# Attention and a dense mixture of experts on one core: on-chip transposes in place of a trip through memory, casting loads from GpSimd, and more of the first expert beside the attention

## The chip, the core and the metric

The kernel runs on one core of a Trainium2 chip. TensorE (PE) does matrix products and transposes and writes PSUM only; PEld is its weight load. VectorE (DVE) and ScalarE (ACT) read PSUM and write SBUF; GpSimd (POOL) works on SBUF. DMA transfers are issued from the queues of SyncE (SP), ACT or POOL and run on 16 DMA engines. The metric is the device time of one execution, in microseconds; lower is better.

## The reference

Four batches of eight heads, 768 positions, 64 numbers a head. Each position attends to a band of 31 neighbours and to 24 block summaries (the maximum of each block of 32 keys, the mean of its values, with a weight of 32). The result, 3072 rows of 512, goes through eight experts, every one on every row, weighted by a matrix P that eight rounds of row and column scaling (Sinkhorn) make from the gate's logits.

```python
mask_l = np.abs(pos[:, None] - pos[None, :]) < window          # window 16
scores_s = scale * np.einsum('bhsd,bhnd->bhsn', q, k_sum) + np.log(block)
...
x = np.ascontiguousarray(attn_out.transpose(0, 2, 1, 3)).reshape(B * S, H * D)
logits = x @ w_gate
P = np.exp(logits)
for _ in range(8):
    P /= P.sum(1, keepdims=True) + 1e-09
    P /= P.sum(0, keepdims=True) + 1e-09
    P *= N / E
for e in range(E):
    out += P[:, e:e + 1] * (np.maximum(x @ w1[e], 0.0) @ w2[e])
```

## The kernel before

**Attention** runs over 16 pairs of heads (`NPAIR`), four pairs to a batch, 128 positions to a tile, six tiles (`G`) to a head. `load_pair` issues six loads of 192 KB in fp32 from SP's queue, two pairs ahead: q, k and v of two heads, 768 rows of 256 bytes each. `cast_qk` and `cast_v` turn them into bf16 on DVE. `transpose_pair` makes 12 transposes on PE; DVE and ACT copy the results out of PSUM, and DVE takes the blockwise maximum of the keys (`ksumT`, L242). `head_scores` makes the band's scores (`sg`, L255, 158 columns a tile) and the summaries' (`ss`, L266); ACT takes exponentials (L260, L271). `head_mask` cuts the band out on POOL (L278). `head_vsum` (L288) sums the values by block. `head_av` (L310), for the pair before, makes 22 small products a head; DVE divides (L313, L314) into `x_sb`.

**The way to the experts.** After four pairs `store_batch` writes the batch's 768 x 512 result to a buffer in device memory, `x_bridge`, and `xbar_batch` reads it back transposed by four DMA transposes into `xT` (L327). `logits_batch` makes the gate's logits.

**Experts.** One step is 512 rows of one expert, six steps (`NG`) an expert, 48 in all. `mm1` makes eight groups of four 512-column matmuls (`hps`, L129) from the pool `fpsum`, which has two buffers, and ACT (L135) and DVE (L138) take turns to apply the relu into `hT`; `mm2` makes four groups of eight (`yps`, L451) for the step before, and DVE adds each group, times P, to `out_acc` (L462). The first two `mm1` of expert 0 (`PREFILL`) are dealt out in small pieces (`mm1_drip`, L149) between the last nine pairs of heads. Weights come in fp32 over SP's queue into one staging buffer (`wst`, 2 MB) and are cast by ACT (L117) or DVE (L119). The Sinkhorn rounds are dealt out over expert 0's steps.

**What sets the order.** Each engine has one queue in order. The code is written pair by pair, and a scheduler in the framework then sets the order within each queue; semaphores between engines do the rest. A DMA's issue waits on its own queue until its buffer is free, and every eighth issue waits for the transfer eight before it.

Of the kernel before, what the change touches and what calls it, by code (L numbers as in the profile page):

```python
# [13 lines left out]
AX = mybir.AxisListType  # L14


@with_exitstack
def kernel(
# [20 lines left out]
    NG = N // 512  # L39
    SCALE = 1.0 / float(D) ** 0.5  # L40
    WIN = 192
    LIVE = 158
    EPL = 112
    EW = EPL + WIN + 80
    NPAIR = (B * H) // 2

    PREFILL = 2
# [3 lines left out]
    dram = ctx.enter_context(tc.tile_pool(name="dram", bufs=1, space=bass.MemoryType.DRAM))  # L51
    fpsum = ctx.enter_context(tc.tile_pool(name="fpsum", bufs=2, space=bass.MemoryType.PSUM))
# [3 lines left out]

    band = const.tile([128, WIN], BF16)
    nc.gpsimd.memset(band, 1.0)
    nc.gpsimd.affine_select(out=band, in_=band, compare_op=ALU.is_ge, fill=0.0,
                            base=-1, pattern=[[1, WIN]], channel_multiplier=-1)  # L60
    nc.gpsimd.affine_select(out=band, in_=band, compare_op=ALU.is_ge, fill=0.0,
                            base=31, pattern=[[-1, WIN]], channel_multiplier=1)

    MBW = 148
    m_big = const.tile([128, MBW], BF16)
    nc.gpsimd.memset(m_big, 1.0)
    nc.gpsimd.affine_select(out=m_big, in_=m_big, compare_op=ALU.is_ge, fill=0.0,
                            base=640, pattern=[[-32, MBW]], channel_multiplier=1)
    nc.gpsimd.affine_select(out=m_big, in_=m_big, compare_op=ALU.is_ge, fill=0.0,
                            base=-609, pattern=[[32, MBW]], channel_multiplier=-1)  # L70
# [17 lines left out]
    wst = [persist.tile([128, 4096], FP32, name=f"wst{i}") for i in range(1)]  # L88
    w1_a = persist.tile([128, KD * F], BF16)
    w2_a = persist.tile([128, KF * DM], BF16)  # L90
    hT_sb = [persist.tile([128, KF, 512], BF16, name=f"hT{i}") for i in range(2)]
    nc.gpsimd.memset(crec_sb, 0.0)

    x_dram = dram.tile([N, DM], BF16, name="x_bridge")

    nc.scalar.dma_start(out=wg_f32[:], in_=moe_w_gate.rearrange("(dk p) e -> p dk e", p=128))
    nc.gpsimd.tensor_copy(out=wg_bf[:], in_=wg_f32[:])

    def load_w1(e, st, part=None):
        src = moe_w1[e].rearrange("(dk p) f -> p dk f", p=128)  # L100
        if part is None:
            nc.sync.dma_start(out=wst[st][:], in_=src)
        else:
            nc.sync.dma_start(out=wst[st][:].rearrange("p (dk f) -> p dk f", dk=KD)[:, part, :],
                              in_=src[:, part, :])

    def load_w2(e, st, part=None):
        src = moe_w2[e].rearrange("(fk p) d -> p fk d", p=128)
        if part is None:
            nc.sync.dma_start(out=wst[st][:], in_=src)  # L110
        else:
            nc.sync.dma_start(out=wst[st][:].rearrange("p (fk d) -> p fk d", fk=KF)[:, 2 * part:2 * part + 2, :],
                              in_=src[:, 2 * part:2 * part + 2, :])

    def cast_w(st, dst, eng):
        if eng is nc.scalar:
            nc.scalar.copy(out=dst[:], in_=wst[st][:])  # L117
        else:
            eng.tensor_copy(out=dst[:], in_=wst[st][:])  # L119

    w1x = [w1_a, None]
    w2x = [w2_a, None]
    hfill = [None]

    def mm1(e, n, fpool, eng2):
        for f in range(KF):
            hp = fpool.tile([128, 512], FP32, tag="h", name="hps")
            for dk in range(KD):
# [348 lines left out]
    for si, (e, n) in enumerate(steps):  # L477
# [14 lines left out]
        if si > 0:  # L492
            mm2(*steps[si - 1])
# [38 lines left out]
```

The softmax here doesn't subtract the row's maximum and nothing guards it: scores larger than these inputs give would overflow.

## Time and profile before

| what | us |
|---|---|
| median of 4 runs | 846.74 (844.48 to 850.33) |
| the profiled execution, its own time | 845.81 |
| its span, first to last instruction | 844.1 |
| last pair's result in `x_sb`, chain | 173.5 |
| `mm1` and `mm2` of one full step, chain | 7.14 and 6.91 |

The profiled execution's time is 1.7 us over its span, and 0.1% under the median. The page cuts the span in 40 slices of 21.1 us: busy shares in tenths, the granted TensorE clock (9 and more is the 2.4 GHz level), and the DMA engines' share. The attention is the first eight or nine slices. The views "by form" group instructions of one line and shape; the chain of waits follows the end of the program back to what released it.

### The profile page before, as it was taken

The page shows a single profiled execution, that of the slowest core. Times are in us where ns is not written, and L with a number is a line of the kernel's source. Part 1 is how long each engine was busy: PE and PEld are TensorE (multiplying, and loading weights), DVE is VectorE, ACT ScalarE, POOL GpSimd, SP SyncE. Part 2 cuts the span into 40 slices and gives each one's busy share as a digit, 9 for nine tenths or more (in the row PEclk, how much of TensorE's full clock was granted, in tenths as well). Part 3 has the DMA queues.
Part 4 walks back from the last instruction along what each step waited for, and adds up shares of the span by engine and source line. Part 5 has one row for each costly group of instructions (what it writes and reads, how often), then busy time and mean ns, then how long its engine had stood idle before and what let it go on. Part 6 is the DMA issues. An engine that isn't in the chain of part 4 may idle for free.

```text
span 844.1 us, 11265 instructions
## 1 busy us (share of the span) xinstructions
PE 788.8 (93%) x4608; PEld 385.7 (46%) x4608; DVE 403.4 (48%) x623; ACT 221.0 (26%) x434; POOL 78.1 (9%) x85
## 2 busy tenths in 40 slices
PE   2876887689999999999999999999999999999998
PEld 1655565544444444444444444444444444444443
DVE  6763676457645445444454454444544544444443
ACT  2644455512131111311311113113111131111110
POOL 6543344400000000000000000000000000000000
PEclk9975698679999999999999999999999999999999
DMA  9979688562022002200220022002200200001122
GB/s 175 173 190 201 161 195 192 142 170 105 0 101 100 1 0 100 100 1 0 100 100 1 0 100 101 1 0 100 100 1 0 101 1 1 0 1 50 55 96 100
DMA packets 107876, 65.76 MB, mean 78 GB/s; under 512 B 89392, under 2 KB 92464, under 8 KB 107824
## 3 DMA queue, kind: packets, MB, share of 16 engines
q1 hardware_dynamic: 104944, 64.43, 27.5%
q10 hardware_dynamic: 2880, 0.61, 0.5%
q8 instruction: 36, 0.59, 0.3%
q14 instruction: 16, 0.13, 0.0%
HBM read 52.45 MB, written 9.44 MB: 73 GB/s over the span
## 4 chain that ended last, share of the span: by engine, by line
PE 85%; DVE 6%; ACT 3%; DMA 2%; issue 2%; SPq 1%; POOL 0%; ACTq 0%; DVEq 0%; POOLq 0%
PE hps L129 38%; PE yps L451 37%; PE av L310 3%; PE hps L149 2%; DMA vvf<-in_v_dram 2%; PE ss L266 1%; PE tk L237 1%; PE sg L255 1%; PE tq L235 1%; DVE kkb L227 1%; ACT kkT L239 1%; DVE ksumT L242 1%; PE vs L288 1%; DVE qqb L226 1%; ACT Esum L271 1%
## 5 line engine op out<-in xcount | busy, mean ns | idle before, releaser
L135 ACT ACTIVATE hT<-hps 128x512 bf16<-128x512 f32 x184 | 109.5, 597 | 496.4 <-PE hps L129 484.3
L451 PEld LDWEIGHTS <-hT 128*128 128x128 bf16 x1536 | 150.1, 98 | 181.0 <-issue 2.7
L138 DVE TENSOR_SCALAR hT<-hps 128x512 bf16<-128x512 f32 x184 | 127.2, 691 | 190.9 <-PE hps L129 190.9
L462 DVE SCALAR_TENSOR_TENSOR out_acc<-yps,P_sb,out_acc 128x512 f32<-128x512 f32 x168 | 125.9, 751 | 153.5 <-PE yps L451 153.5
L129 PE MATMUL hps<-xT,w_b 128*128 128x512 bf16 x768 | 175.9, 378 | 0.3 <-ACT hT L135 0.2
L451 PE MATMUL yps<-w_a,hT 128*128 128x512 bf16 x768 | 174.4, 382 | 0.9 <-DVE xsb L314 0.9
L451 PE MATMUL yps<-w_b,hT 128*128 128x512 bf16 x768 | 170.0, 379 | 0.0
L129 PE MATMUL hps<-xT,w_a 128*128 128x512 bf16 x704 | 163.2, 378 | 0.3 <-DVE hT L138 0.2
L129 PEld LDWEIGHTS <-w_b 128*128 128x128 bf16 x768 | 74.4, 97 | 97.5 <-issue 17.6
L129 PEld LDWEIGHTS <-w_a 128*128 128x128 bf16 x704 | 67.8, 97 | 88.5 <-issue 16.3
L278 POOL TENSOR_TENSOR Et<-Et,band 128x948 bf16<-128x948 bf16 x32 | 66.6, 2083 | 89.7 <-ACT Et L260 88.8
L310 PE MATMUL av<-vsum,Esum 128*128 128x65 bf16 x192 | 34.4, 219 | 10.8 <-DVE xsb L314 7.3
L310 PE MATMUL av<-vve,Et 128*128 128x65 bf16 x512 | 39.0, 220 | 1.0 <-POOL Et L278 1.0
L310 PEld LDWEIGHTS <-Et 128*128 128x128 bf16 x512 | 32.3, 115 | 8.5 <-issue 6.2
L260 ACT ACTIVATE Et<-sg 128x316 bf16<-128x316 f32 x96 | 34.9, 427 | 3.6 <-PE sg L255 3.0
L255 PE MATMUL sg<-qqT,kkT 64*128 64x158 bf16 x192 | 27.7, 292 | 5.2 <-ACT kkT L239 4.9
L266 PE MATMUL ss<-qqT,ksumT 64*128 64x384 bf16 x64 | 23.2, 421 | 6.4 <-DVE ksumT L242 2.9
L271 ACT ACTIVATE Esum<-ss 32x384 bf16<-32x384 f32 x64 | 27.2, 475 | 7.1 <-PE ss L266 7.1
L235 PE MATMUL tq<-ident,qqb 128*128 128x128 bf16 x96 | 11.6, 276 | 17.8 <-DVE qqb L226 17.8
L310 PEld LDWEIGHTS <-Esum 128*128 128x128 bf16 x192 | 21.8, 114 | 13.1 <-PE av L310 7.6
L313 DVE RECIPROCAL recip<-av 128x6 f32<-128x6 f32 x32 | 6.2, 194 | 39.7 <-PE av L310 39.5
L226 DVE CAST qqb<-qqst 128x768 bf16<-128x768 f32 x16 | 22.9, 1433 | 4.2 <-DMA qqst<-in_q_dram 4.2
(73 smaller groups left out, 324.2 us busy)
## 6 DMA issues: line engine op xcount, KB each, us to landing
wst<-in_moe_w_dram SPq DMA_DIRECT2D x14, 2048.0 KB, 8.2
qqst<-in_q_dram SPq DMA_DIRECT2D x32, 192.0 KB, 4.0
out_dram<-out_acc SPq DMA_DIRECT2D x24, 256.0 KB, 2.0
vvf<-in_v_dram SPq DMA_DIRECT2D x31, 192.0 KB, 4.3
kkst<-in_k_dram SPq DMA_DIRECT2D x30, 192.0 KB, 4.0
wst<-in_moe_w_dram SPq DMA_DIRECT2D x8, 512.0 KB, 4.9
x_bridge<-xsb SPq DMA_DIRECT2D x4, 768.0 KB, 5.3
kkst<-in_k_dram ACTq DMA_DIRECT2D x2, 192.0 KB, 5.4
```

The costliest lines, as they stand in the source:

```text
L129: nc.tensor.matmul(hp[:], lhsT=w1x[e % 2][:, dk * F + f * 128:dk * F + (f + 1) * 128], rhs=xT[:, dk, n * 512:(n + 1) * 512], start=(dk == ...
L135: nc.scalar.activation(out=hT_sb[n % 2][:, f, :], in_=hp[:], func=AF.Relu, bias=0.0, scale=1.0)
L138: eng2.tensor_scalar_max(out=hT_sb[n % 2][:, f, :], in0=hp[:], scalar1=0.0)
L226: nc.vector.tensor_copy(out=qq_bf[i % 2][:], in_=qq_st[i % NQKB][:])
L255: nc.tensor.matmul(sg[:, gg, 1:1 + LIVE], lhsT=ktile[p0:p0 + 64, g * 128:(g + 1) * 128], rhs=qtile[p0:p0 + 64, g * 128 + 1:g * 128 + 1 + L ...
L260: nc.scalar.activation(out=et[:, 2 * gp:2 * gp + 2, EPL + 1:EPL + 1 + LIVE], in_=sg[:, :, 1:1 + LIVE], func=AF.Exp, bias=0.0, scale=SCALE)
L266: nc.tensor.matmul(ss[:, :], lhsT=ksumT[i % NTRB][p0:p0 + 64, :], rhs=qtile[p0:p0 + 64, 16 + half * 384:16 + (half + 1) * 384], start=True ...
L271: nc.scalar.activation(out=esum[0:32, half * 384:(half + 1) * 384], in_=ss[0:32, :], func=AF.Exp, bias=0.0, scale=SCALE)
L278: nc.gpsimd.tensor_tensor(out=et[:, :, EPL + 1:EPL + 1 + LIVE], in0=et[:, :, EPL + 1:EPL + 1 + LIVE], in1=band[:, None, 1:1 + LIVE].to_bro ...
L310: nc.tensor.matmul(av[:, c, :], lhsT=lhsT, rhs=rhs, start=(mi == 0), stop=(mi == len(mms) - 1))
L451: nc.tensor.matmul(yp[:], lhsT=hT_sb[n % 2][:, f, t4 * 128:(t4 + 1) * 128], rhs=w2x[e % 2][:, f * DM:(f + 1) * DM], start=(f == 0), stop=( ...
L462: nc.vector.scalar_tensor_tensor(out=out_acc[:, t, :], in0=yp[:], scalar=psl, in1=out_acc[:, t, :], op0=ALU.mult, op1=ALU.add)
```

## The change

The way of one pair is rewritten, and three things move between engines.

- **Loads**: `load` and `load_w` issue from POOL's queue (`nc.gpsimd.dma_start`) with a bf16 destination, so that the transfer casts. The casts on DVE and ACT and the staging buffers go. Pairs still come two ahead, now with three buffers. Expert 0's weights are queued behind pair 3's loads (`gate`), expert 1's behind pair 6's.
- **The mask** goes from POOL to DVE, four instructions a pair (L230), three tiles each.
- **The bridge** through memory goes. `to_xT` transposes a pair's result on PE, six transposes, and ACT copies 128 x 768 into `xT`.
- **Scores**: the two heads of a pair take turns (partitions 0 to 63 and 64 to 127), and the four `ss` products write four strips of 32 partitions of one tile, so one exponential of 128 x 384 takes the place of four of 32 x 384. The block sums of v are made for both heads at once.
- **Fill**: once a batch's `xT` is there, expert 0's whole work on that batch (two halves of 384 rows: eight `hidden` groups and three `project` groups each) is dealt out six pieces a pair through the next four pairs. Three of four batches of expert 0 so lie beside the attention.
- **Experts**: `hidden` draws from `mps2`, four PSUM buffers, `project` from `mps`, three. The Sinkhorn steps lie between the pieces of expert 0's last batch and expert 1's first two steps.

Two places in the queues. The loads: before, on SP's queue, from the end of batch 2 on:

```order
L321 DMA x_bridge<-xsb_151 128x6x512
L211 DMA qqst_113<-in_q_dram 128x6x64
L214 DMA kkst_115<-in_k_dram 128x6x64
L327 DMA_TRANSPOSE xT<-x_bridge 128x768 x4
L211 DMA qqst_113<-in_q_dram 128x6x64
L214 DMA kkst_115<-in_k_dram 128x6x64
L218 DMA vvf_117<-in_v_dram 128x6x64 x2
L112 DMA wst_94<-in_moe_w_dram 128x2x512
```

Now, on POOL's queue, from pair 3's loads on (`w_305` and `w_306` are expert 0's weights, the two copies are the gate):

```order
L183 DMA kst<-in_k_dram 128x6x64 x2
L183 DMA qst<-in_q_dram 128x6x64 x2
L186 DMA vx_112<-in_v_dram 128x6x64 x2
L109 COPY w_305<-kst 1x1
L110 COPY w_306<-kst 1x1
L183 DMA kst<-in_k_dram 128x6x64
L111 DMA w_305<-in_moe_w_dram 128x4x1024
L112 DMA w_306<-in_moe_w_dram 128x8x512
L183 DMA kst<-in_k_dram 128x6x64
```

The loads of q, k and v and the weights have moved from SP's queue to POOL's; pair 4's stand behind 4 MB of weights, and the bridge is gone from between them. The second place is DVE in the middle of the attention, one pair. Before:

```order
L226 CAST qqb_118<-qqst_112 128x768
L227 CAST kkb_120<-kkst_114 128x768
L313 RECIPROCAL recip_147<-av 128x6
L238 COPY qqT_126<-tq 128x384
L314 TENSOR_TENSOR xsb_150<-av,recip_147 128x6x64
L158 TENSOR_SCALAR hT_97<-hps 128x256
L240 COPY qqT_126<-tq 128x384
L242 TENSOR_REDUCE ksumT_132<-kkT_129 128x24
L223 CAST vve_123<-vvf_116 128x780
```

Now (`E_108`, `E_109` are the two heads' exponentials, `h` and `out_acc` belong to the fill):

```order
L230 TENSOR_TENSOR E_108<-E_108,band 128x3x158
L230 TENSOR_TENSOR E_109<-E_109,band 128x3x158
L201 COPY qT_100<-tq 128x768
L202 TENSOR_REDUCE ksT_104<-kT_102 128x24
L125 TENSOR_SCALAR h<-hps 128x384
L244 TENSOR_TENSOR vsx_116<-vs,stripe 128x2x64 x2
L266 RECIPROCAL rec_117<-av 128x6
L267 TENSOR_TENSOR xs<-av,rec_117 128x6x64
L266 RECIPROCAL rec_118<-av 128x6
L267 TENSOR_TENSOR xs<-av,rec_118 128x6x64
L125 TENSOR_SCALAR h<-hps 128x384
L134 COPY out_acc<-yps 128x512
```

The three casts have left DVE's queue; the masks, and the fill's relus and copies, have come in.

```diff
+    wpool = ctx.enter_context(tc.tile_pool(name="wpool", bufs=2))
+    hpool = ctx.enter_context(tc.tile_pool(name="hpool", bufs=2))
+    mps = ctx.enter_context(tc.tile_pool(name="mps", bufs=3, space=PSUM))
...
-    x_dram = dram.tile([N, DM], BF16, name="x_bridge")
...
+    def load_w(e, gate=None):
+        w1 = wpool.tile([128, KD, F], BF16, tag="w1", name="w1")
+        w2 = wpool.tile([128, KF, DM], BF16, tag="w2", name="w2")
+        if gate is not None:
+            nc.gpsimd.tensor_copy(out=w1[0:1, 0, 0:1], in_=gate)
+            nc.gpsimd.tensor_copy(out=w2[0:1, 0, 0:1], in_=gate)
+        nc.gpsimd.dma_start(out=w1[:], in_=moe_w1[e].rearrange("(dk p) f -> p dk f", p=128))
+        nc.gpsimd.dma_start(out=w2[:], in_=moe_w2[e].rearrange("(fk p) d -> p fk d", p=128))
+        w1s[e], w2s[e] = w1, w2
+
...
+    def hidden(e, t0, n, f, h, pool):
+        hp = pool.tile([128, 512], FP32, tag="m", name="hps")
+        for dk in range(KD):
+            nc.tensor.matmul(hp[:, 0:n], lhsT=w1s[e][:, dk, f * 128:(f + 1) * 128],
+                             rhs=xT[:, dk, t0:t0 + n],
+                             start=(dk == 0), stop=(dk == KD - 1))
+        if f % 2 == 0:
+            nc.scalar.activation(out=h[:, f, 0:n], in_=hp[:, 0:n], func=AF.Relu,
+                                 bias=0.0, scale=1.0)
...
+            nc.vector.tensor_scalar_max(out=h[:, f, 0:n], in0=hp[:, 0:n], scalar1=0.0)
+
+    def project(e, t, h, c, pool, raw):
+        yp = pool.tile([128, 512], FP32, tag="m", name="yps")
+        for f in range(KF):
+            nc.tensor.matmul(yp[:], lhsT=h[:, f, c * 128:(c + 1) * 128],
+                             rhs=w2s[e][:, f, :], start=(f == 0), stop=(f == KF - 1))
+        if raw:
+            if t % 2 == 0:
+                nc.vector.tensor_copy(out=out_acc[:, t, :], in_=yp[:])
+            else:
+                nc.scalar.copy(out=out_acc[:, t, :], in_=yp[:])
...
+            nc.vector.scalar_tensor_tensor(out=out_acc[:, t, :], in0=yp[:],
+                                           scalar=P_sb[:, t, e:e + 1], in1=out_acc[:, t, :],
+                                           op0=ALU.mult, op1=ALU.add)
+        if e == E - 1:
+            nc.sync.dma_start(out=out[t * 128:(t + 1) * 128, :], in_=out_acc[:, t, :])
...
+    def first_expert(t0, n, pool):
+
+        h = hpool.tile([128, KF, 512], BF16, tag="h", name="h")
         for f in range(KF):
...
+            yield lambda f=f: hidden(0, t0, n, f, h, pool)
+        for c in range(n // 128):
+            yield lambda c=c: project(0, t0 // 128 + c, h, c, pool, True)
...
+         tc.tile_pool(name="aps", bufs=5, space=PSUM) as aps:
...
+        def load(i):
+            b, h0 = i // PB, (i % PB) * 2
+            qst[i] = attn.tile([128, G, 2, D], BF16, tag="qst", name="qst", bufs=NQ)
+            kst[i] = attn.tile([128, G, 2, D], BF16, tag="kst", name="kst", bufs=NQ)
+            for dst, src in ((kst[i], k), (qst[i], q)):
+                for j in range(2):
+                    nc.gpsimd.dma_start(out=dst[:, :, j, :],
+                                      in_=src[b, h0 + j].rearrange("(g p) d -> p g d", p=128))
...
+                nc.gpsimd.dma_start(out=v_x[i % NQ][:, :, j, 0:D],
+                                    in_=v[b, h0 + j].rearrange("(g p) d -> p g d", p=128))
+
...
+        def transposed(i):
+            r = i % NTR
+            kb, qb = kst.pop(i), qst.pop(i)
+            tk = aps.tile([128, S], BF16, tag="a", name="tk")
...
+            nc.scalar.copy(out=kT[r][:], in_=tk[:])
+            nc.vector.tensor_copy(out=qT[r][:, 16:16 + S], in_=tq[:])
...
+        def scores(i):
+            r = i % NTR
+            for gp in range(2):
+                sg = [aps.tile([128, 3, LIVE], FP32, tag="a", name="sg") for _ in range(2)]
+                for gg in range(3):
+                    g = 3 * gp + gg
+                    for j in range(2):
+                        p0 = 64 * j
+                        nc.tensor.matmul(sg[j][:, gg, :],
+                                         lhsT=kT[r][p0:p0 + 64, g * 128:(g + 1) * 128],
+                                         rhs=qT[r][p0:p0 + 64, g * 128 + 1:g * 128 + 1 + LIVE],
+                                         start=True, stop=True)
+                if gp == 0:
+                    ss = aps.tile([128, HS], FP32, tag="a", name="ss")
+                    for half in range(2):
+                        for j in range(2):
+                            p0, c = 64 * j, 2 * j + half
+                            nc.tensor.matmul(ss[32 * c:32 * c + 32, :],
+                                             lhsT=ksT[r][p0:p0 + 64, :],
+                                             rhs=qT[r][p0:p0 + 64, 16 + half * HS:16 + (half + 1) * HS],
+                                             start=True, stop=True)
+                for j in range(2):
+                    et = E_t[(2 * i + j) % NE][:, 3 * gp:3 * gp + 3, EPL:EPL + LIVE]
+                    nc.scalar.activation(out=et, in_=sg[j][:], func=AF.Exp, bias=0.0, scale=SCALE)
+                    nc.vector.tensor_tensor(out=et, in0=et,
+                                            in1=band[:, None, :].to_broadcast([128, 3, LIVE]),
+                                            op=ALU.mult)
+                if gp == 0:
+                    nc.scalar.activation(out=E_s[i % 2][:], in_=ss[:], func=AF.Exp,
+                                         bias=0.0, scale=SCALE)
+
...
+                nc.vector.tensor_tensor(out=vs_x[i % 2][:, 2 * j:2 * j + 2, 0:D],
+                                        in0=vs[:, j:j + 1, :].to_broadcast([128, 2, D]),
+                                        in1=stripe[:, 2 * j:2 * j + 2, :], op=ALU.mult)
...
+                nc.vector.reciprocal(out=rc[:, :, 0], in_=av[:, :, 64])
+                nc.vector.tensor_tensor(out=xs[:, :, j, :], in0=av[:, :, 0:D],
+                                        in1=rc[:].to_broadcast([128, G, D]), op=ALU.mult)
...
+        def to_xT(i, xs):
+            b, dk = i // PB, i % PB
+            tx = aps.tile([128, S], BF16, tag="a", name="tx")
...
+                nc.tensor.transpose(tx[:, g * 128:(g + 1) * 128],
+                                    xs[:, g, :, :].rearrange("p j d -> p (j d)"), ident)
+            nc.scalar.copy(out=xT[:, dk, b * S:(b + 1) * S], in_=tx[:])
...
+        load(0)
+        const_fills()
...
+        load(1)
...
+        transposed(0)
+        xs = None
+        for i in range(NP):
+            if i + NQ - 1 < NP:
+                load(i + NQ - 1)
+                if i == 1:
+                    load_w(0, kst[3][0:1, 0, 0, 0:1])
+            scores(i)
+            drip(2)
+            if i + 1 < NP:
+                transposed(i + 1)
+            drip(1)
+            vsum(i)
...
+                to_xT(i - 1, xs)
+                if i % PB == 0:
+                    b = i // PB - 1
+                    logits(b)
+                    for half in range(2):
+                        fill += list(first_expert(b * S + half * HS, HS, mps))
+                    if b == 0:
+                        load_w(1)
+            drip(1)
+            xs = values(i)
+            drip(2)
+        to_xT(NP - 1, xs)
+        drip(len(fill))
+
+
+    sps = ctx.enter_context(tc.tile_pool(name="sps", bufs=1, space=PSUM))
+    mps2 = ctx.enter_context(tc.tile_pool(name="mps2", bufs=4, space=PSUM))
+    sink = sps.tile([128, G + 2, E], FP32, name="sink")
...
+    sink_prog = 8 * [sink_rows, sink_cols, sink_recip, sink_bcast, sink_apply]
+
+    def sinkhorn(n):
+        while n > 0 and sink_prog:
+            sink_prog.pop(0)()
+            n -= 1
+
+    b = B - 1
+    for half in range(2):
+        for step in first_expert(b * S + half * HS, HS, mps2):
+            step()
+            sinkhorn(1)
...
+    for si, (e, n) in enumerate(steps):
+        if n == 1 and e + 1 < E:
+            load_w(e + 1)
+        h = hpool.tile([128, KF, 512], BF16, tag="h", name="h")
+        hs[e, n] = h
+        for f in range(KF):
+            hidden(e, 512 * n, 512, f, h, mps2)
+            sinkhorn(1)
+        if si == 1:
+            sinkhorn(len(sink_prog))
+        if si > 0:
+            step2(*steps[si - 1])
+    step2(*steps[-1])
```

## Rows read from the trace of the kernel before

**Rows 1.** The page: span, PE's busy tenths and granted clock in 40 slices.
```profile
span 844.1 us, 11265 instructions
...
PE   2876887689999999999999999999999999999998
...
PEclk9975698679999999999999999999999999999999
```
**Rows 2.** By stretch: length, busy PE, PEld, DVE, ACT, POOL, clock, DMA share, GB/s.
```profile
0.00:21.00 21.00, 5.55 (x47) 4.02 (x48) 12.92 (x12) 5.88 (x15) 14.32 (x55) 1.00 1.03 174
...
42.00:183.00 141.00, 108.71 (x1320) 76.80 (x1316) 77.75 (x151) 67.48 (x191) 52.92 (x26) 0.72 0.73 173
...
285.00:841.00 556.00, 555.02 (x2527) 245.62 (x2524) 238.44 (x322) 110.53 (x161) 0.00 (x0) 1.00 0.13 45
```
**Rows 3.** The chain that ended last: start, length, what; a step, the tail.
```profile
369.06 7.14 PE hps L129 x32
376.20 6.91 PE yps L451 x32
...
840.24 0.75 DVE out_acc L462
```
**Rows 4.** Timeline inside that mm1: start, length, engine; idle before it and releaser.
```profile
370.02 0.60 ACT L135 ACTIVATE hT<-hps 128x512 bf16<-128x512 f32 x1 [8.12 <-PE hps L129]
370.67 0.74 PEld L129 LDWEIGHTS <-w_a 128*128 128x128 bf16 x4 [0.16 <-issue]
```
**Rows 5.** The chain at the attention's end.
```profile
173.46 3.69 DMA x_bridge<-xsb
...
179.69 3.68 DMA xT<-x_bridge
```
**Rows 6.** Timeline, PE's small products of the attention at the full clock.
```profile
101.54 0.22 PE L235 MATMUL tq<-ident,qqb 128*128 128x128 bf16 x1
...
104.66 0.32 PE L266 MATMUL ss<-qqT,ksumT 64*128 64x384 bf16 x1
...
107.33 0.51 PE L235 MATMUL tq<-ident,qqb 128*128 128x128 bf16 x6
```
**Rows 7.** The chain: one head's 22 products at the two clock levels.
```profile
114.87 0.68 PE av L310 x22
...
171.24 1.38 PE av L310 x22
```
**Rows 8.** Groups by line and shape, attention and relu: busy, mean ns, idle before, releaser.
```profile
L138 DVE TENSOR_SCALAR hT<-hps 128x512 bf16<-128x512 f32 x184 | 127.2, 691 | 190.9 <-PE hps L129 190.9
...
L278 POOL TENSOR_TENSOR Et<-Et,band 128x948 bf16<-128x948 bf16 x32 | 66.6, 2083 | 89.7 <-ACT Et L260 88.8 <-ACT Esum L271 0.9
...
L260 ACT ACTIVATE Et<-sg 128x316 bf16<-128x316 f32 x96 | 34.9, 427 | 3.6 <-PE sg L255 3.0
...
L314 DVE TENSOR_TENSOR xsb<-av,recip 128x384 bf16<-128x384 f32 x32 | 17.8, 556 | 0.9
...
L242 DVE TENSOR_REDUCE ksumT<-kkT 128x24 bf16<-128x768 bf16 x16 | 15.2, 951 | 6.1 <-ACT kkT L241 5.7
...
L158 DVE TENSOR_SCALAR hT<-hps 128x256 bf16<-128x256 f32 x16 | 6.7, 422 | 8.0 <-PE hps L149 7.5 <-ACT Esum L271 0.4
...
L313 DVE RECIPROCAL recip<-av 128x6 f32<-128x6 f32 x32 | 6.2, 194 | 39.7 <-PE av L310 39.5
```
**Rows 9.** DMA issues: count, KB each, median us to landing.
```profile
wst<-in_moe_w_dram SPq DMA_DIRECT2D x14, 2048.0 KB, 8.2
qqst<-in_q_dram SPq DMA_DIRECT2D x32, 192.0 KB, 4.0
```
**Rows 10.** Timeline of the start: DVE's first cast, POOL's last memset, pair 1's transposes.
```profile
5.57 8.65 DVE L226 CAST qqb<-qqst 128x768 bf16<-128x768 f32 x1 [4.23 <-DMA qqst<-in_q_dram]
...
13.62 0.19 POOL L199 MEMSET vsum<- 128x65 bf16 x1
...
20.29 0.83 PE L235 MATMUL tq<-ident,qqb 128*128 128x128 bf16 x6
```

More of the change, by code (lines that the diff above doesn't have):

```diff
@@ L14 @@
 AX = mybir.AxisListType
+PSUM = bass.MemoryType.PSUM
 @with_exitstack
@@ L61 @@
[L61 to L70, printed above, removed]
+    band = const.tile([128, LIVE], BF16)
@@ L115, in cast_w @@
[L115 to L125, printed above, removed]
-        for f in range(KF):
-            hp = fpool.tile([128, 512], FP32, tag="h", name="hps")
-            for dk in range(KD):
-                nc.tensor.matmul(
-                    hp[:],
-                    lhsT=w1x[e % 2][:, dk * F + f * 128:dk * F + (f + 1) * 128],
-                    rhs=xT[:, dk, n * 512:(n + 1) * 512],
-                    start=(dk == 0), stop=(dk == KD - 1))
-            if f % 2 == 0:
-                nc.scalar.activation(out=hT_sb[n % 2][:, f, :], in_=hp[:],
-                                     func=AF.Relu, bias=0.0, scale=1.0)
-            else:
-                eng2.tensor_scalar_max(out=hT_sb[n % 2][:, f, :], in0=hp[:],
-                                       scalar1=0.0)
@@ L402, with drip @@
-    lgm = mpsum.tile([128, G, E], FP32, name="lgm", tag="lgm")
-    def logits_batch3():
+                    nc.tensor.matmul(lp[:, t6, :], lhsT=xT[:, dk, t * 128:(t + 1) * 128],
+                                     rhs=wg_bf[:, dk, :],
+                                     start=(dk == 0), stop=(dk == KD - 1))
+            nc.vector.tensor_copy(out=logits_sb[:, b * G:(b + 1) * G, :], in_=lp[:])
+        fill = []
+        def drip(n):
+            while n > 0 and fill:
+                fill.pop(0)()
+                n -= 1
@@ L468 @@
[L468 to L495 removed]
+                                in1=rrec_sb[:].to_broadcast([128, NT, E]), op=ALU.mult)
@@ new lines, with step2 @@
+    last_logits()
+    p_init()
+    sink_prog = 8 * [sink_rows, sink_cols, sink_recip, sink_bcast, sink_apply]
+    def sinkhorn(n):
+        while n > 0 and sink_prog:
+            sink_prog.pop(0)()
+            n -= 1
+    b = B - 1
[3 more added lines that the diff above has]
+            sinkhorn(1)
+    hs = {}
+    pools = [mps2, mps]
+    steps = [(e, n) for e in range(1, E) for n in range(N // 512)]
+    def step2(e, n):
+        h = hs.pop((e, n))
+        for c in range(4):
+            t = 4 * n + c
+            if e == 1:
@@ L496 @@
                 nc.vector.tensor_scalar_mul(out=out_acc[:, t, :], in0=out_acc[:, t, :],
                                             scalar1=P_sb[:, t, 0:1])
-    while sink_i < len(sink_prog):
-        sink_prog[sink_i]()
-        sink_i += 1
-    mm2(*steps[-1])
+            project(e, t, h, c, mps, False)
+    for si, (e, n) in enumerate(steps):
[10 more added lines that the diff above has]
+            step2(*steps[si - 1])
```

439 lines of the change are left out of this document (107 added, 332 removed).

## The prediction

> **What bounds the kernel now.** I read the page's slices first: PE is busy nine tenths or more from the tenth slice on, at the full clock, and only six to eight tenths in the slices before, where the clock falls to the 1.2 GHz level in parts [rows 1]. The table by stretch says the same in numbers: from 285 to 841 us PE is busy 555 of 556 us, so the experts are bound by PE alone; from 42 to 183 us it is busy 109 of 141 at a mean clock of 0.72, DVE 78, ACT 67, POOL 53 and the DMA engines 73% [rows 2]. There no engine is full: the stretch is bound by the loads and by waits that go from engine to engine. Then the chain. In the experts it is PE without a gap, but a step's `mm1` takes 7.14 us and its `mm2`, with as many columns, 6.91 [rows 3]. The timeline shows why: ACT ends the first group's relu at 370.62, and PE loads the third group's weights at 370.67 after a wait of 0.16; two PSUM buffers are one too few [rows 4]. At the attention's end the chain leaves PE for the bridge: write from 173.46, the last transpose landed at 183.4, 9.9 us [rows 5].
>
> So the program is an attention of 183 us and 661 us of experts. The profiled time is 845.8, 1.7 over the span of 844.1, 0.1% under the median; my sum is made against that time.
>
> **The experts after the change.** 6.91 us is 32 matmuls of 512 columns, 0.216 each [rows 3]. Experts 1 to 7 are 42 steps. With four PSUM buffers for `hidden` the relu of group f has three groups' time, 2.6 us, where it needs 0.7 [rows 8]; I take 6.91 for both halves: 42 x 13.82 = 580.4 us. The 0.23 that each `mm1` loses now is worth 9.7 of that. Expert 0's last batch stays behind the attention: 64 matmuls of 384 columns at 0.162 and 48 of 512 at 0.216, 20.8 us. The Sinkhorn rounds: PE waits for DVE twice in each of eight rounds, with a piece of expert work put between. Bounds: 0, if the piece covers it, and 8, if each round costs PE one DVE reduction of 0.95 [rows 8]; I take 3, with the last logits, since the pieces of 0.65 to 1.7 us are about as long as the reductions. The tail, last add and store, is as now: 844.1 - 840.24 = 3.9 [rows 3]. Sum: 580.4 + 20.8 + 3 + 3.9 = 608 us. The weights' two transfers an expert have 70 us to land; two of the same size from SP take 8.2 each [rows 9]. The casts that go (ACT, DVE) were off the path, and nothing there is late next: DVE has four relus and four adds a step, under 6 of 13.8 us [rows 2, 8].
>
> **The attention's work per pair.** PE at the full clock: a train of six transposes takes 0.51 where one takes 0.22, so 0.058 each [rows 6]; 18 of them are 1.04. The 44 value products are 2 x 0.68 [rows 7], the block sums six of 128 columns, 0.35. The band's 12 products at 158/512 of 0.216 are 0.8, the summaries' four at 0.162 0.65. With the logits, some 0.2, that is 4.4 us. The fill adds a quarter of 20.8, 5.2 us: 9.6 a pair. DVE: masks of 474 columns at the reduction's 1.24 ns a column (951 ns for 768, [rows 8]), 0.59 each, 2.4 for four; from below half of that, if DVE takes two bf16 numbers a cycle. No row shows a bf16 product on DVE out of SBUF; I take the upper value because the nearest row, the reduction, is bf16 from SBUF too. The copy of q, 0.95 at most, the maximum 0.95, two small products at a reciprocal's 0.2, reciprocals and divisions 2 x 0.75, relus two of 384 columns at 0.56 (between 422 and 691 ns), copies 0.5. Sum 7.8 us, under PE's 9.6. ACT at 1.35 ns a column (427 for 316, [rows 8]): four exponentials of 474, one of 384, two copies of 768, two relus, 0.75 copies: 6.7 at most. POOL loses 4.2 us of masks a pair. The bridge's four round trips go off the DMA engines, and its 9.9 us at the end go off the path; in their place stand six transposes and a copy, about 2 us.
>
> **The loads.** Six of 192 KB a pair, now issued from POOL. No row shows a load from POOL. Bounds for the pace p of one load: 1.13 us, which is 192 KB at the 174 GB/s of the first 21 us with the DMA engines full [rows 2], and 4.0, the median from issue to landing [rows 9], as if none overlapped another. I take the lower: up to eight may be under way, and SP's queue reached that pace with the same 256-byte rows. That hides them behind 10.7 us a pair (6 x 1.13 = 6.8), but not at the start: pair 4's loads are queued behind expert 0's weights. The first load landed at 5.57 [rows 10]; 29 more are 32.8 us, the weights 2 x 8.2 [rows 9], so pair 4 starts at about 54. Pairs 0 to 3 fit in before that. A gain I don't price: DVE's first cast took 8.65 us, until POOL's memsets ended at 13.81 [rows 10]; those casts go, and pair 1 still waits for its loads.
>
> That row bears on a rule against this change. The Trainium skill, page "SBUF — State Buffer", section "SBUF: two separate sides", says that DVE and GpSimd share a pair of SBUF ports as an exclusive lock, so that loads issued from GpSimd starve while DVE copies within SBUF. The row agrees on the lock. By the rule in its hardest reading the masks' 2.4 us would be added to POOL's 6.8 a pair, 9.2, still under 10.7: the sum would not move.
>
> **Pairs with fill.** Pairs 4 to 15: PE's 9.6 plus what waits are left. The chain from scores to values is five ACT exponentials, at most 3.1 us, and two masks, 1.2; between them PE has transposes, block sums and fill pieces of about 3.5. I take 1.1 of waiting, 10.7 a pair: 128 us. Bounds: 9.6 (all covered) and 12.5 (DVE's 7.8 with relus and copies of the fill ahead of the masks in its queue). End of the attention: 54 + 128 + 2 = 184. The span: 184 + 608 = 792; with 1.7, **794 us**. Against before: the attention as long as now, and the experts 53 shorter. Range of this case: 768 (first fill pair at 40, when the weights take a gap in the loads, 9.6 a pair) to 816 (12.5 a pair).
>
> **Rivals.**
>
> *The loads go at POOL's pace.* Pair 1's transposes stand at about 21 us as now (20.29, [rows 10]); after that 15 pairs at 6p: time = 21 + 90p + 2 + 608 + 1.7 = 633 + 90p. Up to p = 1.78 nothing changes; at 2.38 the kernel is where it was; at the 4.0 of [rows 9] it is 993 us. For it: one engine now makes every issue, 768 rows each, in one queue, and each row is half the bytes when it is written. Against it: SP's pace, and POOL has nothing else to do. I give 0.12 to a pace between 1.78 and 2.38 (795 to 845 us) and 0.17 to a slower one, the side on which the change loses.
>
> The skill's page "DMA: Bandwidth & Descriptors", section "Anatomy of one DMA — SWDGE (gpsimd) path", fits such transfers with 2.0 us plus bytes over 436 GB/s; by that, an estimate, 2.45 us each, and by the sum above 853 us if none overlapped. No run here shows it yet.
>
> *The fill isn't covered.* If PE keeps the 0.72 clock of the attention now [rows 2], a fill pair is 9.6 / 0.72 + 1.1 = 14.4: 54 + 173 + 2 + 608 + 1.7 = 839. For it: the attention's waits, which leave the clock low in the slices now. Against: the slices with nine tenths busy have the full clock [rows 1], and the fill brings PE to 9.6 of 10.7. Chance 0.09.
>
> **How the numbers follow.** The forecast 0.60, loads 0.12 and 0.17, fill 0.09, 0.02 for anything else. The range of 768 to 855 leaves out the slow loads and a little below. A measurement tells about 0.5% from no change, here 842.5 to 851. Faster: 0.60 + 0.11 + 0.08 = 0.79; same 0.03; slower 0.18.
>
> **What would show it.** In the changed kernel: steps of 13.8 us and no PE wait at `hidden`; the first expert's batches 0 to 2 ahead of 185 us; clock near 1 from about 55 us; DVE under 8 us a pair; PE's waits in the attention on ACT and DVE, not on loads. A PE that waits for `kst` in every pair would be the first rival; a clock near 0.7 after pair 4 the second. A step much over 13.8, for a reason I don't see, would break the largest term.

## The result, and the profile after

The changed kernel takes 769.84 us (768.70 to 772.01), 0.909 of the time before, 95% interval 0.907 to 0.912. The profiled execution has a span of 770.0. Forecast were 794 for the time and 792 for the span, in a range of 768 to 855. The page after, the rows that answer to [rows 1]:

```profile
span 770.0 us, 10721 instructions
...
PE   2689999999999999999999999999999999999997
...
PEclk9879999999999999999999999999999999999999
```

PE is at nine tenths or more from the fourth slice on, where it took ten before, and the clock is at its 2.4 GHz level almost everywhere. By stretch (length, busy PE, PEld, DVE, ACT, POOL, clock, DMA share, GB/s; compare [rows 2]):

```profile
0.00:54.00 54.00, 29.87 (x398) 22.45 (x399) 29.65 (x72) 19.95 (x36) 44.63 (x74) 0.87 1.47 118
54.00:160.00 106.00, 105.40 (x1357) 68.28 (x1356) 72.79 (x172) 57.91 (x110) 43.23 (x53) 1.00 0.92 71
200.00:765.00 565.00, 565.00 (x2619) 256.01 (x2618) 245.41 (x353) 95.52 (x160) 8.18 (x10) 1.00 0.15 29
```

From 54 us on the attention is bound by PE, which is busy in 105.4 of 106 us at clock 1.00, against 108.7 of 141 at 0.72 before [rows 2]. The chain (start, length, what) shows one step of the experts and the last add; the source view of the last batch's logits (kernel line, count, shortest, median and longest in ns, first and last start) tells where the attention ends:

```profile
206.40 6.91 PE hps L118 x32
213.31 6.91 PE yps L130 x32
...
765.88 0.75 DVE out_acc L138
```
```profile
L344 PE MATMUL sink<-wg_bf,xT x24: 166/166/169, 160.4 to 161.0; 128*128 128x8 bf16 x24
```

So the attention ends at 160.4 us and what follows takes 609.6, against 184 and 608 in the forecast. What PE still waits for lies almost all in the first 54 us (us in total, times, longest; the last row is from the Sinkhorn rounds), the timeline has the place (start, length, instruction, idle before and its releaser), and the chain has the load that pair 4 waits for:

```profile
PE tk L194 <- DMA kst<-in_k_dram: 9.5, 2, 6.2
PE hps L118 <- DMA w<-in_moe_w_dram: 6.2, 1, 6.2
PE tq L198 <- DMA qst<-in_q_dram: 3.5, 3, 1.8
...
PE sink L360 <- DVE csum_sb L356: 0.4, 2, 0.3
```
```profile
21.05 1.72 POOL L183 DMA_DIRECT2D kst<-in_k_dram  x2
22.67 1.74 POOL L183 DMA_DIRECT2D qst<-in_q_dram  x2
...
42.38 1.64 POOL L183 DMA_DIRECT2D qst<-in_q_dram  x2 [5.18 <-DMA w<-in_moe_w_dram]
```
```profile
35.81 0.48 PE L118 MATMUL hps<-xT,w 128*128 128x384 bf16 x1 [6.25 <-DMA w<-in_moe_w_dram]
...
39.93 0.58 PE L214 MATMUL sg<-qT,kT 64*128 64x158 bf16 x6
...
50.11 0.57 PE L214 MATMUL sg<-qT,kT 64*128 64x158 bf16 x6
```
```profile
30.21 13.76 DMA qst<-in_q_dram
```

POOL issues a load every 0.81 us. At 35.81 PE has stood 6.25 us at a product of the fill, for the first expert's weight; 39.93 and 50.11 are the scores of pairs 3 and 4. Pair 4's q, issued behind the weights by 30.21, lands 13.76 us later, at 43.97. The q at 42.38 is pair 5's, whose issue has waited 5.18 us for the weights.

### The profile page after: what moved, and what is told of

The parts are those of the page before. It is cut to its first block, busy times and chain, and to the rows that moved or that the text cites. A ratio compares the mean times of both kernels' runs of the same rounds, so it can differ in the third digit from the quotient of the medians.

```text
span 770.0 us, 10721 instructions
## 1 busy us (share of the span) xinstructions
PE 740.6 (96%) x4608; PEld 366.9 (48%) x4608; DVE 374.9 (49%) x663; ACT 184.8 (24%) x326; POOL 97.7 (13%) x138
## 4 chain that ended last, share of the span: by engine, by line
PE 90%; DVE 3%; POOL 3%; DMA 2%; ACT 1%; issue 1%; ACTq 0%; POOLq 0%; DVEq 0%
PE yps L130 43%; PE hps L118 40%; PE av L263 3%; DMA qst<-in_q_dram 2%; PE sg L214 1%; DVE h L125 1%; POOL qst L183 1%; POOL kst L183 1%; PE tq L198 0%; DVE ksT L202 0%; PE vs L240 0%; PE tx L275 0%; POOL vx L186 0%; PE ss L223 0%; ACT E L229 0%
## 5 line engine op out<-in xcount | busy, mean ns | idle before, releaser
L118 PE MATMUL hps<-xT,w 128*128 128x512 bf16 (+1 forms) x1600 | 348.6, 372 | 7.1 <-DMA w<-in_moe_w_dram 6.2
L130 PE MATMUL yps<-w,h 128*128 128x512 bf16 x1536 | 340.9, 379 | 0.0
L118 PEld LDWEIGHTS <-w 128*128 128x128 bf16 x1600 | 153.9, 98 | 177.0 <-issue 8.0
L130 PEld LDWEIGHTS <-h 128*128 128x128 bf16 x1536 | 149.6, 98 | 178.5
L122 ACT ACTIVATE h<-hps 128x512 bf16<-128x512 f32 (+1 forms) x200 | 116.2, 581 | 488.5 <-PE hps L118 488.4
L125 DVE TENSOR_SCALAR h<-hps 128x512 bf16<-128x512 f32 (+1 forms) x200 | 133.8, 669 | 166.8 <-PE hps L118 165.3
L229 ACT ACTIVATE E<-sg 128x474 bf16<-128x474 f32 x64 | 33.2, 581 | 38.7 <-PE sg L214 38.7
L230 DVE TENSOR_TENSOR E<-E,band 128x474 bf16<-128x474 bf16 x64 | 25.8, 411 | 9.9 <-ACT E L229 8.5
L183 POOL DMA_DIRECT2D kst<-in_k_dram x32 | 27.0, 863 | 26.8 <-PE tk L194 16.0
L186 POOL DMA_DIRECT2D vx<-in_v_dram x32 | 27.0, 870 | 10.8 <-PE av L263 10.4
L183 POOL DMA_DIRECT2D qst<-in_q_dram x32 | 27.0, 872 | 5.2 <-DMA w<-in_moe_w_dram 5.2
```

The source lines that it names most:

```text
L118: nc.tensor.matmul(hp[:, 0:n], lhsT=w1s[e][:, dk, f * 128:(f + 1) * 128], rhs=xT[:, dk, t0:t0 + n], start=(dk == 0), stop=(dk == KD - 1))
L122: nc.scalar.activation(out=h[:, f, 0:n], in_=hp[:, 0:n], func=AF.Relu, bias=0.0, scale=1.0)
L125: nc.vector.tensor_scalar_max(out=h[:, f, 0:n], in0=hp[:, 0:n], scalar1=0.0)
L130: nc.tensor.matmul(yp[:], lhsT=h[:, f, c * 128:(c + 1) * 128], rhs=w2s[e][:, f, :], start=(f == 0), stop=(f == KF - 1))
L183: nc.gpsimd.dma_start(out=dst[:, :, j, :], in_=src[b, h0 + j].rearrange("(g p) d -> p g d", p=128))
L186: nc.gpsimd.dma_start(out=v_x[i % NQ][:, :, j, 0:D], in_=v[b, h0 + j].rearrange("(g p) d -> p g d", p=128))
```

## The experiments

The differences below are ratios to the kernel before, measured beside each run, times the 846.64 us of before; the changed kernel is 769.9 on that scale.

**Two PSUM buffers.**

```diff
-    mps2 = ctx.enter_context(tc.tile_pool(name="mps2", bufs=4, space=PSUM))
+    mps2 = ctx.enter_context(tc.tile_pool(name="mps2", bufs=2, space=PSUM))
```

> The changed kernel with two PSUM buffers for the hidden products of the experts instead of four, nothing else. Theory (the 0.23 us that each first half lost before came from a third product group finding no free buffer): 42 steps lose 0.23 each, 9.7 us, so about 780, and the chain shows 7.14 beside 6.91 again. Rival (the new order of the code, hidden products of one step ahead of the projection of the step before, is what took the 0.23 away): 770, and 6.91 stays.

783.74 us, ratio 0.924 (0.921 to 0.927), 12 us more. The chain of a step:

```profile
236.84 7.20 PE hps L118 x32
244.04 6.91 PE yps L130 x32
```

0.29 a step comes back, a little more than the 0.23 expected, and the second half stays at 6.91; 42 x 0.29 = 12.2. The theory holds.

**No fill in the attention.** The pieces wait in their list until the pairs are through; expert 0's weights come behind the last loads.

```diff
-            while n > 0 and fill:
+            while n > 0 and fill and late:
...
-                if i == 1:
-                    load_w(0, kst[3][0:1, 0, 0, 0:1])
+                if i == NP - 3:
+                    load_w(0, kst[NP - 1][0:1, 0, 0, 0:1])
```

> The changed kernel with the first expert's work on batches 0 to 2 held back until the attention is over; its weights are loaded with the last pairs. Theory (from pair 4 on PE is full, so the fill only takes the place of waits that would otherwise be shorter): a pair without fill goes down from 9.2 us to what DVE and POOL need, 5.2 us of work each, so 5.2 to 6.5, the attention ends at 105 to 125, the 62 us of fill follow, and the whole is 773 to 795. Rival (the pairs take 9 us anyway, for their chain of waits, and the fill lies in them for nothing): 62 us more, about 830.

783.51 us, ratio 0.923 (0.920 to 0.926), 11 us more. The stretch in the middle, rows of the chain from the scores of one pair to those of the next, and PE's wait for the weight:

```profile
54.00:78.00 24.00, 20.31 (x397) 15.94 (x394) 20.50 (x53) 15.88 (x31) 24.00 (x30) 1.00 1.90 122
```
```profile
71.19 0.31 PE sg L214 x6
...
73.83 0.63 DVE E L230 x2
...
74.66 0.88 DVE ksT L202
...
75.80 0.85 PE av L263 x22
76.64 0.31 PE sg L214 x6
```
```profile
PE hps L118 <- DMA w<-in_moe_w_dram: 7.2, 1, 7.2
```

A pair without fill takes 5.45 us, and PE is busy in 20.3 of 24 us. What bounds the pair there is its chain, from the scores over the transposes and DVE's masks and maxima to the values. The loads are not in that chain, though the stretch has POOL busy in 24.0 of 24 us: its issues start 0.81 us apart, six of them in 4.9 us, and their records overlap. The last logits start at 172.2. PE stands 7.2 us of that for the weight, and in the 12 us behind it its clock is 0.76, which costs some 3 more; without both it would be about 162 (an estimate, not run), where the changed kernel has 160.4. So of the 62 us of fill in the pairs only about 11 are a gain: the fill covers the weights' load, and otherwise takes the place of pairs that would run faster. The theory holds. The run is not the fill alone, since no weights stand ahead of pair 4 here: its scores start at 37.8 instead of 50.1.

**Masks on GpSimd.**

```diff
-                    nc.vector.tensor_tensor(out=et, in0=et,
+                    nc.gpsimd.tensor_tensor(out=et, in0=et,
```

> The changed kernel with the band's mask on GpSimd again, four instructions a pair. Theory (GpSimd's queue is the loads' queue): four masks of about 1.04 us (half of the 2.08 of the double size before) and six issues of 0.86 make 9.4 us a pair on GpSimd against 9.2 of PE, so GpSimd becomes the bound, with waits: 772 to 800. Rival (DVE's masks hold up the loads that GpSimd issues, by a shared port): issues and landings get shorter and the time goes below 768.

792.65 us, ratio 0.934 (0.932 to 0.937), 21 us more. PE's wait, the stretch, and the groups on POOL (busy, mean ns):

```profile
PE av L263 <- POOL E L230: 10.2, 14, 1.6
```
```profile
54.00:165.00 111.00, 102.51 (x1240) 65.70 (x1241) 50.50 (x114) 53.46 (x102) 98.94 (x108) 0.92 0.97 75
```
```profile
L230 POOL TENSOR_TENSOR E<-E,band 128x474 bf16<-128x474 bf16 x64 | 67.8, 1118 | 13.1 <-ACT E L229 13.1
...
L183 POOL DMA_DIRECT2D kst<-in_k_dram x32 | 27.4, 864 | 2.6 <-DMA w<-in_moe_w_dram 2.6
```

Four masks of 1.12 and six issues of 0.86 fill POOL, 98.9 of 111 us. The values wait for masks, 10.2 us in all, and PE's clock is 0.92 over the stretch, for 1.00 in the changed kernel. An issue takes 0.86 us, as in the changed kernel (0.863). The theory holds.

**Loads from SP with casts.**

```diff
+            for dst, src, eng in ((kst[i][:], k, nc.vector), (qst[i][:], q, nc.vector),
+                                  (v_x[i % NQ][:, :, :, 0:D], v, nc.gpsimd)):
+                st = attn.tile([128, G, 2, D], FP32, tag="f32", name="f32st", bufs=6)
+                for j in range(2):
+                    nc.sync.dma_start(out=st[:, :, j, :], ...)
+                eng.tensor_copy(out=dst, in_=st[:])
...
```

> The changed kernel with q, k and v loaded in fp32 from SP's queue, as before, six loads of the same rows a pair, and cast on DVE (q, k) and GpSimd (v). Theory (from pair 4 on PE is full and the loads only set the start): DVE gets two casts of about 0.95 more, 9 of 9.2 us, the first 30 loads come at about 1.1 us instead of 0.83, so the fill starts up to 9 us later: 772 to 790. Rival (the casting loads are themselves a main part of the gain, since they take DVE and ACT off the pair's path): above 800.

775.48 us, ratio 0.914 (0.911 to 0.917), 4 us more, in the start: PE waits 11.2 us for casts of q. The last logits are at 164.7 for 160.4. The theory holds; the casting loads of q, k and v are a small part of the gain. The weights still come by casting loads from POOL in this run.

**The way through memory.**

```diff
-            for g in range(G):
-                nc.tensor.transpose(tx[:, g * 128:(g + 1) * 128], ...)
-            nc.scalar.copy(out=xT[:, dk, b * S:(b + 1) * S], in_=tx[:])
+            nc.sync.dma_start(out=x_dram[...], in_=xs[...])
+            if dk == PB - 1:
+                for g in range(KD):
+                    nc.sync.dma_start_transpose(out=xT[:, g, b * S:(b + 1) * S], in_=x_dram[...])
```

> The changed kernel with the way through memory put back: each pair's result is written to a buffer in device memory, and after four pairs four DMA transposes bring it into xT, all from SP's queue; PE makes no transposes of the result. Theory (the round trip costs its 10 us once, where nothing covers it, behind the last pair; PE saves 16 x 0.35 of transposes): 770 + 10 - 6, so 772 to 780. Rival (the DMA transposes get in the way of the loads, which share the engines, in every batch): 10 us a batch, above 790.

789.21 us, ratio 0.931 (0.927 to 0.936), 18 us more: between the two. The chain:

```profile
27.35 11.05 DMA x_bridge<-xs
38.42 8.68 DMA xT<-x_bridge
...
54.26 5.20 DMA x_bridge<-xs
59.54 9.69 DMA xT<-x_bridge
...
97.90 4.37 DMA x_bridge<-xs
102.33 2.81 DMA xT<-x_bridge
```

The round trip takes 15 to 20 us in the first batch, beside weights and loads, and 7 later. PE waits 18.1 us in all, most of it there; at the end the fill left over covers it (PE is busy in 14.9 of the 15 us to 180). Neither theory had that place. That the weights' transfer is what stretches the first round trips is inferred from their time, not tested.

**No masks.**

```diff
-                    nc.vector.tensor_tensor(out=et, in0=et,
-                                            in1=band[:, None, :].to_broadcast([128, 3, LIVE]),
-                                            op=ALU.mult)
```

> The changed kernel without the four masks a pair on DVE (the band is not cut out, so the output differs). Theory (PE from pair 4 on, GpSimd's issues and the transfers before that; DVE has room): 765 to 771. Rival (DVE's queue, or its hold on a port that GpSimd needs for the loads, sets the pace in part): up to 16 x 1.64 = 26 us less, below 760.

This kernel leaves the band uncut. 769.68 us, ratio 0.909 (0.904 to 0.914): no difference. Issue to landing of k's loads from 54 to 160 us, in this kernel and then in the changed one (count, KB, median us):

```profile
kst<-in_k_dram POOLq DMA_DIRECT2D x16, 96.0 KB, 3.4
```
```profile
kst<-in_k_dram POOLq DMA_DIRECT2D x17, 96.0 KB, 3.5
```

26 us of DVE's work gone change nothing beyond the interval, 4 us either way. DVE does not bound the attention, and its masks do not hold up the loads.

**One head after the other.**

```diff
-                for gg in range(3):
-                    g = 3 * gp + gg
-                    for j in range(2):
+                for j in range(2):
+                    for gg in range(3):
+                        g = 3 * gp + gg
```

> The changed kernel with the scores of the two heads one head after the other, as before, instead of taking turns. Theory (products on different partition strips overlap on PE, which is why twelve band products take 0.62 us in the changed kernel and four summary products 0.27, where one after the other they would be 0.80 and 0.65): 0.56 us a pair in the twelve pairs that PE bounds, 776 to 779. Rival (each product takes its columns, whatever its neighbour): 770.

771.96 us, ratio 0.911 (0.907 to 0.915): no difference. The timeline of this kernel:

```profile
110.36 0.39 PE L214 MATMUL sg<-qT,kT 64*128 64x158 bf16 x6
110.67 0.34 PE L223 MATMUL ss<-qT,ksT 64*32 64x384 bf16 x4
110.95 0.39 PE L214 MATMUL sg<-qT,kT 64*128 64x158 bf16 x6
111.27 1.48 PE L118 MATMUL hps<-xT,w 128*128 128x384 bf16 x8
```

From start to start six products take 0.31 us and four 0.28; with turns, in the changed kernel from 112.41 us on, it is 0.31 and 0.27. The theory falls, and so does the rival's reason, since six times 158 columns one by one are 0.40 at 0.216 for 512. The products overlap in either order; what sets how far stays open.

**A quicker start, and the order of the sum.** Four kernels change the first 50 us: e8_start has the first two pieces of the diff, e9_reversed the last, e10_start_reversed all, and e11_merged_v_reversed the last two.

```diff
+                if i < EARLY:
+                    nc.gpsimd.dma_start(out=dst[:].rearrange(...).rearrange("p (j m) -> p j m", j=2),
+                                        in_=src[b, h0:h0 + 2].rearrange("j (p g) d -> p j (g d)", p=128))
...
                 if i == 1:
-                    load_w(0, kst[3][0:1, 0, 0, 0:1])
+                    load_w1(0, kst[3][0:1, 0, 0, 0:1])
+                if i == 2:
+                    load_w2(0, kst[4][0:1, 0, 0, 0:1])
...
-        for dk in range(KD):
+        for dk in reversed(range(KD)):
```

> The changed kernel with a quicker start: for the first six pairs q and k come with six neighbouring rows on a partition (1536 bytes in a piece, one load for both heads, 24 transposes of 64 columns and a copy that puts the columns in order), v's two loads are one, the constants are made behind pair 1's loads, and the first expert's second weight comes behind pair 4's loads instead of pair 3's. Theory (until pair 4 the loads' issues on GpSimd, 0.83 us each, and the 4 MB of weights in front of pair 4 set the pace): about half of the 24 first issues go and 1 MB steps back, the fill starts 8 to 14 us sooner, 756 to 763. Rival (the transfers themselves, not their issues, or PE's clock in the start, set it): 767 to 771.

> The changed kernel with the four parts of each hidden product added up in reverse order, pair 3's first, nothing else. In the changed kernel the framework sets the fill's first products, which need only the first pairs' rows, ahead of pair 2's values in PE's queue, where PE stands 6.25 us for the first expert's weights. In reverse the fill can't begin before pair 3 is through. Theory (that stall sets back pairs 2 and 3 and so the start): the wait for the weights goes, pair 4 starts at about 46 us, when its loads have landed, instead of 50: 764 to 767. Rival (pair 4's loads, queued behind 4 MB of weights, set the start whatever PE does before): 769 to 771.

> The quicker start of e8_start together with the reverse order of e9_reversed. Theory (in e8_start the issues were cheaper, 0.72 us for two heads, but PE stood 12.05 us for the first weight in front of pair 2's values, and GpSimd's queue stood behind PE for a free buffer of v): without that stall pairs 2 and 3 run at 17 to 30 us and pair 4 starts at 32 to 40: 752 to 762. Rival (the transfers of weights and loads before pair 4 are what takes the time): 766 to 770.

> As e10_start_reversed, but q and k loaded in rows of 256 bytes as in the changed kernel; only v's two loads are one, the constants come behind pair 1's loads and the second weight behind pair 4's. Theory (pieces of 1536 bytes take less of the DMA engines and of GpSimd): the start is 4 to 8 us later than in e10_start_reversed, 758 to 766. Rival (the size of the pieces doesn't count in the start): the same as e10_start_reversed.

e8_start: 768.54 us, 0.907 (0.903 to 0.912). e9_reversed: 773.69, 0.912 (0.908 to 0.915). e10_start_reversed: 764.22, 0.901 (0.897 to 0.904). e11_merged_v_reversed: 770.64, 0.907 (0.904 to 0.911). PE's wait in e8_start, and its waits for k in e9_reversed:

```profile
31.78 0.48 PE L127 MATMUL hps<-xT,w 128*128 128x384 bf16 x1 [12.05 <-DMA w<-in_moe_w_dram]
```
```profile
PE tk L194 <- DMA kst<-in_k_dram: 19.1, 3, 9.5
```

Alone, each edit moves a wait: e8_start's earlier pairs stand 12.05 us for the weight instead of 6.25 (768.5 lies in the rival's range), and in e9_reversed the 6.25 are gone and PE waits 19.1 us for k instead of 9.5. There the rival was right, if a little low (771.8 on the scale above): the loads queued behind the weights set the start. Together they leave no wait for the weights, and 10 us of waits for q, k and v, of which 5.2 lie ahead of the first load's landing. Pair 4's scores in e10_start_reversed, and its issues of one load for two heads:

```profile
37.18 0.38 PE L236 MATMUL sg<-qT,kT 64*128 64x158 bf16 x6
```
```profile
14.59 0.73 POOL L192 DMA_DIRECT2D qst<-in_q_dram  x1
15.30 0.73 POOL L192 DMA_DIRECT2D kst<-in_k_dram  x1
```

Pair 4 starts at 37.2 instead of 50.1, but pair 5 at 50.1, so the attention ends 4.6 us sooner (last logits at 155.8). It is the fastest of all, 7 us under the changed kernel, though short of the 752 to 762 that I expected. Rows of 1536 bytes, with one issue for two heads, are worth 5 to 6 of it: e11_merged_v_reversed, which lacks them, is not clearly faster than the changed kernel.

**Four parts back at once**: the edits of e1_psum2, e3_maskpool, e4_spload and e5_bridge together.

> The changed kernel with four parts put back at once, each as in its own run: two PSUM buffers for the hidden products (e1_psum2), the masks on GpSimd (e3_maskpool), fp32 loads from SP with casts on DVE and GpSimd (e4_spload), and the way through memory (e5_bridge). What stays of the change is the order of the code: the fill in the pairs, whole batches of the first expert, and the joint exponential. By their ratios to the kernel before (0.924, 0.934, 0.914 and 0.931 against 0.909) they cost 12, 21, 4 and 19 us alone. Theory (each is a wait or a piece of work of its own in front of a PE that is otherwise full, so they add up): 770 + 56 = 826, between 818 and 834; the last 20 us to the kernel before belong to the order of the code. Rival A (they cover one another: the masks wait under the bridge, GpSimd is free of the loads' issues once SP has them): below 815. Rival B (one part makes another worse): above 838.

799.47 us, ratio 0.945 (0.939 to 0.951), 30 us more: rival A. PE's waits for the masks are gone:

```profile
PE av L265 <- POOL E L232: 0.2, 1, 0.2
...
PE lp L288 <- DMA xT<-x_bridge: 19.6, 5, 17.3
```

With these loads on SP, POOL has only the masks, the casts of v and the weights' few issues, and the 21 us of e3_maskpool vanish: they were the price of masks and issues in one queue. The bridge's wait does not merely hide them: from 80 to 165 us, behind its longest part, PE is busy in 83.6 of 85 us. Left are the bridge's wait, the PSUM buffers and the start.

## Why the prediction came out as it did

**The experts (right).** 608 forecast, 609.6 measured. Steps are 6.91 + 6.91, and the two buffers were the cause (e1_psum2). Without the 42 steps, 25.1 us lie between the last logits and the last add (765.88 - 580.4 - 160.4), for 23.8 forecast: logits and Sinkhorn rounds cost 4 instead of 3. They are not the waits that I had in mind, since PE waits 0.4 us for DVE there; what is left is mostly the rounds' own small products. The tail is 4.1 for 3.9.

**The start (right in size, partly by luck).** Pair 4's scores start at 50.1, where I had pair 4 at 54. The loads' pace of 1.13 us, my lower bound, was too slow: POOL issues one in 0.81 to 0.87. The weights held pair 4's q up by about 10 us (13.8 from issue to landing, where 3.8 is the median of q's loads), not by 16.4. So it had landed at 44, and the loads' sum was 10 us too long. The 6 us from there to the scores I had left out: pair 4's transposes, pair 3's values at the 1.2 GHz level, and fill between. I had also expected PE's waits on ACT and DVE; they are on loads and weights. Not foreseen was that PE itself would stand at a fill product ahead of pair 2's values; e9_reversed, without that stall, is no faster, since pair 4's q lands no sooner (43.9).

**The pair with fill (mis-sized).** This is the step that failed: 10.7 us taken, 9.2 measured ((160.4 - 50.1) / 12), 18 of the 22 us of the miss; 4 come from the start, and the 2 I had added for the last pair are gone, against 2 more behind. 9.2 is also under the 9.6 that I had for a pair with everything covered. The time stays in the range, by 2 us, because the range's lower end let pair 4 begin at 40 us besides (that end sums to 767, not 768): the bound on the pair was too high, the one on the start too early, and the two errors offset each other. "I take 1.1 of waiting" was wrong: PE is busy 105.4 of 106 us. And PE's own 9.6 was too much: scores take 0.9 us a pair (0.62 + 0.28) where I had 0.8 + 0.65 for products one by one. DVE is at 6.3 a pair (72.8 of 106 us), not 7.8: a mask takes 0.41, in the middle of my 0.29 to 0.59. Taking the upper value for the mask did no harm, as DVE does not bound (e6_nomask).

**Where the gain was put (wrong as a cause).** "The attention as long as now, and the experts 53 shorter": the attention is 23 us shorter and the rest 51. And e2_nofill shows that the fill is not what brings the 51: without it the experts' part grows by 62 and the pairs shrink by nearly as much, but for the weights' load. What brings the gain is an attention whose pair could go in 5.45 us where it took about 11 before (16 in 173 us, [rows 5]). PE's rows to the end of the attention, before and after, say where it shows:

```profile
0.00:183.00 183.00, 133.02 (x1589) 95.01 (x1589) 105.57 (x188) 86.72 (x243) 78.14 (x85) 0.79 0.79 173
```
```profile
0.00:160.00 160.00, 135.27 (x1751) 90.73 (x1752) 102.44 (x243) 77.86 (x145) 87.86 (x126) 0.96 1.10 87
```

PE is busy for as long as before, though it now does 62 us of the first expert's work there instead of 14: it works at a mean clock of 0.96 instead of 0.79, and idles 25 us instead of 50. Of the whole gain of 77 us, e12_four_back says, bridge, masks, loads of q, k and v, and buffers account for 30; the other 47 lie in what that run keeps: the order of the code with the fill, the weights' casting loads, the joint exponential and the rest of the rewritten pair. I did not take these apart, so which of them takes the waits away stays open.

**The bridge (wrong place).** I counted 9.9 us at the end. e5_bridge costs 18, most of it in the first batch, where the round trip runs beside the weights' transfer.

**The masks (left out).** I listed that POOL loses 4.2 us of masks and gave it no price. e3_maskpool prices it at 21, because POOL issues the loads now; in e12_four_back, where it does not, PE waits 0.2 us for masks.

**The rivals.** Loads at POOL's pace: issues start 0.81 us apart, in e2_nofill too, less than half of the 1.78 from which the pace would count. The Trainium skill's fit, page "DMA: Bandwidth & Descriptors", section "Anatomy of one DMA — SWDGE (gpsimd) path", gave 2.45 us by my estimate; the trace has 3.5 to 4 from issue to landing, and several under way at once, so the sum of 853 did not come. The fill not covered: the clock is 1.00 from 54 us. The Trainium skill's rule of the shared port, page "SBUF — State Buffer", section "SBUF: two separate sides", is about DVE's copies; the masks are products of two tensors. Neither moving them from DVE nor leaving them out made an issue or a landing of k shorter beyond 0.1 us, so nothing of it shows for them here.

## To carry to other kernels

Price a part that leaves an engine by who else is in that engine's queue afterwards: the same masks cost 21 us beside the loads' issues and next to nothing without them. Before crediting work that is moved under another stage, ask how fast that stage would run without it; when the same engine serves both, the move is worth only the waits it fills. A stall that is taken away at the start shows the next one, so change what both wait for together. And an engine that a row shows busy all the time is the bound only if the chain goes through it.

## What the runs showed of the hardware that I had not expected

An issue on GpSimd takes longer with the number of rows, not of bytes: 0.73 us for 256 rows of 1536 bytes, 0.76 for the 512 rows of the first weight (2 MB in fp32), 0.82 to 0.87 for 768 rows of 256 bytes, 0.89 for the 1024 rows of the second weight, and 1.02 for 1536 rows of 256 bytes, v's merged load in e10_start_reversed:

```profile
12.88 1.02 POOL L198 DMA_DIRECT2D vx<-in_v_dram  x1
```

And while PE stood 6.25 us (to 35.81), its clock fell to the 1.2 GHz level. Products ran at that level until about 41 us, at the full clock until about 44.5, and, after shorter waits there, at the 1.2 GHz level again until 51 us: six score products take 0.58 us at 39.93 and 0.57 at 50.11, for 0.38 at 112.41; six transposes take 0.49 at 42.85. The stretch of the changed kernel (columns as above, clock 0.66), the transposes and the later products:

```profile
35.00:54.00 19.00, 15.04 (x184) 11.17 (x185) 8.88 (x23) 7.20 (x14) 11.73 (x15) 0.66 1.78 144
```
```profile
42.85 0.49 PE L194 MATMUL tk<-ident,kst 128*128 128x128 bf16 x6 [0.88 <-ACT E L229]
...
112.41 0.38 PE L214 MATMUL sg<-qT,kT 64*128 64x158 bf16 x6
```
